# Two early tiles leave the six rotating PSUM banks, and the opening order is written anew

## The chip, the cores and the metric

The kernel runs on one core of one Trainium2 chip. The metric is the device time of one execution in microseconds (us), the median of three runs. A profile is one more execution, taken by the hardware profiler; its span runs from the first to the last instruction. The engines: TensorE (PE for matmuls, PEld for the weight loads that go beside them), VectorE (DVE), ScalarE (ACT), GpSimd (POOL), and SyncE (SP), which here only issues DMAs.

## The reference

A gated recurrence over 768 positions, for 4 batches and 8 heads, feeds a two-layer feed-forward network of 3072 tokens:

```
# recurrence, in chunks of 32: L[i,j] = exp(cum_i - cum_j) for i >= j, else 0
y_intra = (C @ B.T * L) @ x
y_inter = (C @ state) * exp(cum)
state   = exp(sum(log a)) * state + (B * exp(cum_last - cum)).T @ x
# network, d_model 256, d_ff 2048, on the recurrence's output
h   = y @ w_in
out = softplus(h) @ w_out
```

## The kernel before

**Tiling.** The positions are cut into 6 units u of 128, for all batches. A unit becomes 512 tokens of the network. The network's hidden side is cut into 16 slices k of 128. For each of the 96 pairs (j, k) there is a *first* (F: six matmuls of 512 columns, `w_in` times x, into a PSUM tile `hp`), then ACT's Softplus into `e`, its high part `gh` (ACT) and the rest `gl` (DVE), and a *second* (Z: two times three matmuls into the accumulators `acc0`, `acc1`). All network products are split into high and low float32r parts, three matmuls for each product.

**The recurrence of a unit.** Each unit has two halves p. The words of one half: D (four decay masks `rm`, written by POOL from factors `fc`), S (scores, PE, four PSUM tiles `sp`), M (four products of `sp` and `rm`, DVE), I (within, PE, into `yp`). Then B, U, T, N carry the state, C and R read it, G multiplies `yp` by growths `gg` (DVE), Xh and Xl split the result into `xh` (ACT) and `xl` (DVE), which the firsts read. H1 and H0 are halves of unit 0's first two F, that need only half of its tokens.

**Weights.** A word w*n* loads 512 KB of raw weights (SP); six words W*n* turn them into high and low parts, with four steps on ACT (`w`, two of `signs`, `wih` or `woh`) and two on DVE (`w`, `wil` or `wol`). Four buffers `wraw` hold the raw weights, so that a later load waits until ACT has read an earlier one.

**Order.** Nearly everything up to the 32nd F and the 28th Z is a list of words, `ORDER` (line 61), replayed with every instruction kept in its engine's order; later units are placed by `FILLS`. Each engine works through its own queue in order and waits on semaphores.

**PSUM.** There are eight banks. Six belong to the pool `ps` (line 129) and rotate under one tag: `zeros`, `fp`, `total`, `log_sums`, `sp`, `hp` and others take the next free one. Two belong to `pa` (line 130): the accumulators `acc0` and `acc1`, which unit 0's `yp` and two of the growths' tiles borrow through `early_bank` (line 213) before the first Z.

**The opening.** `la`, `lb`, `kb` load logs and constants; `loga` takes logarithms; `ft0` multiplies them by summing matrices (`fp0` and `total0`, lines 321 to 339) and exponentiates into `fc` and `ft`; `warm` (line 298) issues matmuls of zeros into `zeros`; `gc` and `gq` make unit 0's growths on chip (`log_sums`, `by_head_row`, `gp`); `gd` and `gg1` take the other units' growths through DRAM; `us` and `ux` load the rows and tokens of unit 0, `un` those of a later one.

Of the kernel before, what the change touches and what calls it, by code (L numbers as in the profile page):

```python
# [10 lines left out]
F32 = mybir.dt.float32  # L11
# [10 lines left out]
P = 128  # L22
# [36 lines left out]


ORDER = """
la loga lb logr warm6 loga ft0 logr ft0 ft0 warm1 ft0 ft0 ft0 kb growth logb gb D0.0.0 growth gc us0.0 w0 S0.0 D0.0.1
gc warm1 M0.0.0 W0 ux0.0 D0.0.2 M0.0.2 gq M0.0.1 D0.0.3 us0.1 M0.0.3 fr0 W0 gq B0.0 W0 logb ux0.1 D0.1.0 warm1 gq
growth gq fr0 W0 W0 I0.0 S0.1 ft1 w2 B0.1 D0.1.3 G0.0 gq fr0 M0.1.0 Xh0.0 D1.0.2 D0.1.1 M0.1.3 ft1 D0.1.2 M0.1.1
M0.1.2 D1.0.3 ft1 fr1 fr1 un1.0 U0 W2 W0 w4 Xl0.0 fr0 I0.1 w1 ft1 G0.1 W2 W2 D1.1.0 fr1 W2 N0 S1.0 W4 fr1 Xh0.1 W4 H1
D1.0.1 Xl0.1 H0 M1.0.1 D1.1.3 W2 W2 M1.0.2 W4 F0.1 W4 tl F0.0 W1 W4 gd P0.0 F0.2 un1.1 D1.0.0 P0.2 M1.0.0 w6 W1 T1
F0.3 P0.1 M1.0.3 w3 D1.1.2 S1.1 W1 B1.0 P0.0 B1.1 P0.1 W4 M1.1.0 W1 W1 un2.0 F0.5 W3 P0.2 D1.1.1 P0.0 W1 F0.4 P0.5 W3
M1.1.1 P0.1 Z0.0 gg1 M1.1.2 W6 Z0.1 M1.1.3 W6 W3 W6 P0.4 C1 P0.5 P0.2 P0.4 W3 U1 P0.3 W3 w7 I1.0 W6 N1 w5 I1.1 W3 R1
W6 G1.0 w12 Xh1.0 W6 G1.1 W7 P0.3 P0.3 S2.0 Z0.2 F0.7 w9 W5 W7 W7 D2.0.0 M2.0.0 Xh1.1 un3.0 w8 F0.6 W5 P0.4 Xl1.0
Xl1.1 W5 Z0.3 D2.0.3 P0.6 M2.0.3 W5 W5 B2.0 D2.0.1 W5 F1.4 P0.6 F1.0 Z0.4 P0.7 M2.0.1 un2.1 F1.7 F1.1 F1.3 P0.7 W7 W8  # L70
P0.5 W7 P1.0 W7 W12 Z0.5 B2.1 F1.2 w10 W8 P0.6 W8 W12 W12 P1.0 P1.1 P0.7 Z0.6 Z0.7 P1.4 W12 W12 P1.4 P1.1 P1.0 F1.5
K0.1 P1.1 P1.2 K0.0 W12 W8 D2.0.2 P1.2 W8 W8 P1.4 Z1.0 F1.6 P1.5 Z1.1 W10 W10 W9 W10 P1.2 P1.6 W10 F0.9 W10 P1.5 w14
P1.7 W10 P1.5 P1.3 Z1.2 P1.3 P1.3 W9 D2.1.2 P1.7 W9 P1.7 W9 W9 W9 P0.9 T2 F0.10 C2 F0.13 P0.13 W14 Z1.3 P0.13 Z1.4 w11
W11 W11 P1.6 P1.6 W11 W11 F0.12 D2.1.0 w15 F0.11 W14 W14 w13 F0.8 Z1.5 W14 W11 P0.13 W11 W14 P0.12 P0.9 W14 F1.8 P0.10
P0.9 W13 P0.8 Z1.6 F1.12 F0.14 P0.10 P0.10 P0.14 W13 W15 Z1.7 F0.15 P0.8 P0.8 F1.13 K1.1 K1.0 W13 W15 W13 W15 M2.0.2
W15 P0.11 W15 Z0.8 Z0.9 gg2 W13 P0.11 Z0.10 P0.14 P0.14 W15 P0.15 F1.9 F1.10 P0.11 P0.12 P1.9 W13 P0.12 Z0.11 Z0.12
P0.15 P1.9 D3.0.0 P1.10 P1.9 Z0.13 P0.15 P1.8 P1.8 Z0.14 Z0.15 P1.10 E0 D2.1.1 F1.14 D2.1.3 F1.11 D3.0.2 P1.8 P1.12
P1.14 Z1.8 P1.14 S2.1 P1.10 M2.1.3 M2.1.1 M2.1.0 Z1.9 M2.1.2 P1.12 U2 P1.11 P1.11 P1.14 N2 P1.12 P1.13 I2.0 I2.1 P1.11
S3.0 M3.0.0 R2 G2.1 D3.0.1 Z1.10 G2.0 M3.0.1 P1.13 M3.0.2 Xh2.1 F1.15 P1.13 un3.1 Xl2.1 D3.0.3 Z1.11 Xh2.0 P1.15 P1.15
Xl2.0 M3.0.3 gg3 P1.15  # L80
"""
HALF = NFT // 2
AHEAD = 32
# [37 lines left out]
def recurrence_then_ffn(ctx: ExitStack, tc: tile.TileContext, un, alr, w_in, w_out, const, outT):  # L121
# [7 lines left out]
    ps = ctx.enter_context(tc.tile_pool(name="ps", bufs=6, space=PSUM))  # L129
# [30 lines left out]
    kb = cp.tile([P, C_END], F32, name="kb")  # L160
# [8 lines left out]
    gd = dr.tile([NH, NU * RT], F32, name="gd")  # L169
# [43 lines left out]
    def early_bank(e, name):  # L213
        return pa.tile([P, 512], F32, tag=f"acc{e}", name=name)
# [81 lines left out]
    zeros = []  # L296

    def warm(n):
        if not zeros:
            zeros.append(ps.tile([P, 512], F32, tag="ps", name="zeros"))  # L300
        for _ in range(n):
            PE.matmul(
                zeros[0][:32].rearrange("p (a b) -> p a b", b=32),
                some,
                some.unsqueeze(1).broadcast_to([P, 16, 32]),
                start=True,
                stop=True,
            )
# [12 lines left out]
    def factors_by_token(g):  # L321
        logs = first_logs[:, : NS * NR] if g == 0 else lo
        n = logs.shape[1]
        fp = ps.tile([P, 512], F32, tag="ps", name=f"fp{g}")
        for i in range(NC):
            PE.matmul(fp[:, i * n : (i + 1) * n], kc[:, i * P : (i + 1) * P], logs, start=True, stop=True)
        yield
        by_chunk = fp[:, : NC * n].rearrange("p (c k) -> p c k", c=NC)
        total = None
        for a, b in ((0, NR), (NR, n)) if g == 0 else ((0, n),):  # L330
            cols = slice(g * NS * NR + a, g * NS * NR + b)
            A.activation(fc[:, cols].rearrange("p k c -> p c k"), by_chunk[:, :, a:b], AF.Exp)
            yield
            if total is None:
                total = ps.tile([P, 512], F32, tag="ps", name=f"total{g}")[:, :n]
                PE.matmul(total, kc[:, NC * P : K_END], logs, start=True, stop=True)
                yield
            A.activation(ft[:, cols], total[:, a:b], AF.Exp)
            yield
# [408 lines left out]
    def constants_on_chip():  # L748
# [3 lines left out]
    acts = {  # L752
        "init": constants_on_chip,
        "warm": warm,
        "la": lambda: load(first_logs, alr[:, : (NS + 1) * NR]),
        "lb": lambda: load(other_logs, alr[:, (NS + 1) * NR :]),
# [12 lines left out]
        "logr": staged(lambda: log_clipped(lr)),  # L769
        "growth": staged(growth),  # L770
        "ft": staged(factors_by_token),
        "fr": staged(factors_by_row),
        "W": staged(split_stages),
# [112 lines left out]
```

## Time and profile before

| | us |
|---|---|
| runs, median of 3 (lowest to highest) | 313.52 (313.27 to 314.02) |
| profiled execution | 313.66 |
| its span, first to last instruction | 312.0 |
| PE busy (98% of the span) | 307.1 |
| ACT busy (54%) | 169.0 |
| DVE busy (50%) | 154.7 |
| POOL busy (13%) | 41.5 |

The engines other than PE do most of their work in the first third: the tenths of ACT's busy time are 9 in slices 4 to 6 of 40 and fall to 3 and 4 after slice 18. A matmul's end is modelled, so the time between the starts of neighbouring matmuls tells more than a busy share of 9 or 10 tenths.

### The profile page before, as it was taken

How to read it: one execution, taken by the hardware profiler on the slowest of the kernel's cores; microseconds unless marked ns; L12 is line 12 of the kernel's file. 1: busy time of each engine (PE TensorE's matmuls, PEld its weight loads, DVE VectorE, ACT ScalarE, POOL GpSimd, SP SyncE). 2: the span in 40 equal slices, each digit the busy share in tenths (PEclk: the TensorE clock that was granted, in tenths of full speed). 3: DMA queues.
4: the chain of work that ended last, by engine and by line, in shares of the span. 5: the costliest groups of instructions: out<-in, count | busy, mean ns of one | idle time of the engine just before them, and what ended most of it. 6: DMA issues, size and time to landing. Idle time of an engine off the chain costs nothing.

```text
span 312.0 us, 5683 instructions
## 1 busy us (share of the span) xinstructions
PE 307.1 (98%) x2325; PEld 251.9 (81%) x2325; DVE 154.7 (50%) x264; ACT 169.0 (54%) x292; POOL 41.5 (13%) x55
## 2 busy tenths in 40 slices
PE   8999999999999999999999999999999999999995
PEld 5787888888788888888888888888888888888884
DVE  5999793647444973553922252642352332322222
ACT  4899897988855254244344534344534344534450
POOL 2780600004410531000300000300000000000000
PEclk9999999999999999999999999999999999999999
DMA  7997664240004550000610100000100000100001
GB/s 214 406 373 178 237 235 137 63 137 2 2 0 152 165 193 35 35 1 2 237 35 0 69 0 0 4 0 0 67 4 0 2 0 2 67 0 0 2 0 67
DMA packets 10442, 24.37 MB, mean 78 GB/s; under 512 B 1072, under 2 KB 1840, under 8 KB 10416
## 3 DMA queue, kind: packets, MB, share of 16 engines
q1 hardware_dynamic: 10416, 24.01, 22.9%
q8 instruction: 18, 0.29, 0.4%
q14 instruction: 8, 0.07, 0.1%
HBM read 20.76 MB, written 3.24 MB: 77 GB/s over the span
## 4 chain that ended last, share of the span: by engine, by line
PE 91%; ACT 3%; DVE 3%; issue 1%; POOL 1%; POOLq 0%; DVEq 0%; ACTq 0%
PE acc L141 40%; PE hp L141 39%; PE yp L141 5%; PE sp L141 4%; ACT signs L141 1%; PE zp L141 1%; PE end L141 1%; DVE rm L141 1%; PE zeros L141 1%; DVE gl L141 1%; ACT gh L141 1%; PE fp L141 1%; ACT e L141 1%; POOL rm L141 1%; DVE wil L141 0%
## 5 line engine op out<-in xcount | busy, mean ns | idle before, releaser
L655 DVE TENSOR_TENSOR gl<-e,gh 128x512 fp32r<-128x512 f32 x54 | 37.3, 692 | 92.0 <-ACT gh L652 92.0
L141 PE MATMUL hp<-xh,wih 128*128 128x512 f32 (+1 forms) x196 | 75.7, 386 | 0.0
L141 PE MATMUL hp<-xl,wih 128*128 128x512 f32 (+1 forms) x196 | 75.4, 385 | 0.0
L141 PE MATMUL hp<-xh,wil 128*128 128x512 f32 (+1 forms) x196 | 75.4, 385 | 0.0
L141 PE MATMUL acc<-gh,woh 128*128 128x512 f32 x188 | 74.3, 395 | 0.1
L649 ACT ACTIVATE e<-hp 128x512 f32<-128x512 f32 x54 | 32.3, 599 | 77.6 <-PE hp L141 77.3
L141 PE MATMUL acc<-gl,woh 128*128 128x512 f32 x188 | 73.3, 390 | 0.0
L141 PE MATMUL acc<-gh,wol 128*128 128x512 f32 x188 | 73.2, 389 | 0.0
L141 DVE TENSOR_TENSOR gl<-e,gh 128x512 fp32r<-128x512 f32 x42 | 30.3, 731 | 32.8 <-ACT gh L141 32.8
L141 PEld LDWEIGHTS hp<-xh,wih 128*128 128x128 f32 x196 | 36.8, 188 | 7.5
L141 PEld LDWEIGHTS hp<-xh,wil 128*128 128x128 f32 x196 | 36.8, 188 | 7.4
L141 PEld LDWEIGHTS hp<-xl,wih 128*128 128x128 f32 x196 | 36.8, 188 | 7.3
L141 POOL TENSOR_SCALAR_AFFINE_SELECT rm<-fc 128x512 f32<-128x512 f32 x36 | 32.2, 929 | 77.0 <-ACT signs L141 41.9
L141 PEld LDWEIGHTS acc<-gh,woh 128*128 128x128 f32 x188 | 35.3, 188 | 8.7 <-ACT signs L141 0.5
L141 PEld LDWEIGHTS acc<-gh,wol 128*128 128x128 f32 x188 | 35.3, 188 | 7.4
L141 PEld LDWEIGHTS acc<-gl,woh 128*128 128x128 f32 x188 | 35.3, 188 | 7.2 <-DVE gl L655 0.2
L141 ACT ACTIVATE e<-hp 128x512 f32<-128x512 f32 x42 | 24.6, 592 | 22.0 <-PE hp L141 17.3
L652 ACT CAST gh<-e 128x512 fp32r<-128x512 f32 x54 | 33.5, 621 | 4.1 <-PE acc L141 2.4
L141 ACT CAST gh<-e 128x512 fp32r<-128x512 f32 x42 | 25.6, 616 | 12.9 <-PE acc L141 12.4
L141 DVE TENSOR_TENSOR rm<-sp,rm 128x512 f32<-128x512 f32 x32 | 20.7, 683 | 5.3 <-PE sp L141 5.2
L141 ACT ACTIVATE signs<-wraw 128x512 f16<-128x512 f32 (+1 forms) x32 | 23.3, 781 | 0.0
L405 POOL TENSOR_SCALAR_AFFINE_SELECT rm<-fc 128x512 f32<-128x512 f32 x12 | 8.7, 754 | 81.4 <-PE yp L141 69.4
(105 smaller groups left out, 209.5 us busy)
## 6 DMA issues: line engine op xcount, KB each, us to landing
un<-in_un SPq DMA_DIRECT2D x10, 768.0 KB, 6.0
wraw<-in_w_in SPq DMA_DIRECT2D x8, 512.0 KB, 5.2
wraw<-in_w_out SPq DMA_DIRECT2D x8, 512.0 KB, 5.3
gg<-gd SPq DMA_DIRECT2D x20, 128.0 KB, 3.8
out_t<-o SPq DMA_DIRECT2D x9, 256.0 KB, 2.1
head_in_h<-in_un SPq DMA_DIRECT2D x2, 384.0 KB, 4.9
head_in_l<-in_un SPq DMA_DIRECT2D x2, 384.0 KB, 6.3
out_t<-half SPq DMA_DIRECT2D x2, 256.0 KB, 2.2
```

The costliest lines, as they stand in the source:

```text
L141: return lambda *a, **k: tc.keep_in_program_order(f(*a, **k))
L405: Pl.affine_select(out=weights_of(u, p, ks.start, ks.stop).rearrange("p h (c i) -> p (h c) i", i=SUB), in_=fs.rearrange("p h c -> p (h c)" ...
L649: A.activation(e, h, AF.Softplus)
L652: A.copy(gh, e)
L655: V.tensor_tensor(gl, e, gh.bitcast(F32), op=ALU.subtract)
```

## The change

`zeros` and `total0` are taken from the two accumulator banks instead of the six rotating ones, and the word list is another one. The nine matmuls of zeros all stand ahead of `gq`, since `gp0` takes the bank of `zeros`. Line 335 (the second factors' `total1`) stays in the rotating pool.

```diff
 ORDER = """
-la loga lb logr warm6 loga ft0 logr ft0 ft0 warm1 ft0 ft0 ft0 kb growth logb gb D0.0.0 growth gc us0.0 w0 S0.0 D0.0.1
...
+warm6 la loga lb loga logr logb ft0 logr us0.0 growth growth kb gb ft0 ft0 ft0 ft0 S0.0 ft0 D0.0.0 w0 M0.0.0 gc gc
...
     def warm(n):
         if not zeros:
-            zeros.append(ps.tile([P, 512], F32, tag="ps", name="zeros"))
+            zeros.append(early_bank(0, "zeros"))
...
             if total is None:
-                total = ps.tile([P, 512], F32, tag="ps", name=f"total{g}")[:, :n]
+                total = (ps.tile([P, 512], F32, tag="ps", name="total1") if g else early_bank(1, "total0"))[:, :n]
                 PE.matmul(total, kc[:, NC * P : K_END], logs, start=True, stop=True)
```

From unit 3 on (`FILLS`), and in the last 798 rows of PE's queue, both programs have the same order. Three places of the new order matter below.

The first is the opening on PE and DVE. Before, on PE, from the first factors' `total` to the first scores (`sp` of unit 0, first half, four tiles):

```order
L141 MATMUL total_124<-first_logs,kc 128x128
L141 LDWEIGHTS some
L141 MATMUL zeros<-some 32x512
L141 MATMUL log_sums<-kc,first_logs 32x128 x4
L141 MATMUL sp_00_148<-head_in_h 128x128
L141 MATMUL sp_01_149<-head_in_h 128x128
L141 MATMUL sp_02_150<-head_in_h 128x128
L141 MATMUL sp_03_151<-head_in_h 128x128
```

Now, on PE, the end of those scores and what follows them:

```order
L141 MATMUL sp_00_137<-head_in_h 128x128
L141 MATMUL sp_01_138<-head_in_h 128x128
L141 MATMUL sp_02_139<-head_in_h 128x128
L141 MATMUL sp_03_140<-head_in_h 128x128
L141 MATMUL log_sums<-kc,first_logs 32x128 x4
L141 LDWEIGHTS some
L141 MATMUL zeros<-some 32x512
```

The scores now come straight behind `total`; `log_sums` and three matmuls of zeros (of which the first stands here) moved behind them. On DVE, before, around the same scores (`by_head_row` reads `log_sums`; the four rows of `rm` are the words M0.0):

```order
L141 SCALAR_TENSOR_TENSOR other_logs<-cum 128x192
L141 COPY by_head_row<-log_sums 128x128
L141 TENSOR_TENSOR rm_0_137<-sp_00_148,rm_0_137 128x512
L141 TENSOR_TENSOR rm_0_137<-sp_02_150,rm_0_137 128x512
L141 TENSOR_TENSOR rm_0_137<-sp_01_149,rm_0_137 128x512
L141 TENSOR_TENSOR rm_0_137<-sp_03_151,rm_0_137 128x512
```

And now:

```order
L141 COPY own<-kb 128x256
L141 TENSOR_TENSOR rm_0_158<-sp_00_137,rm_0_158 128x512
L141 COPY by_head_row<-log_sums 128x128
L141 TENSOR_TENSOR rm_0_158<-sp_01_138,rm_0_158 128x512
L141 TENSOR_TENSOR rm_0_158<-sp_02_139,rm_0_158 128x512
L141 TENSOR_TENSOR rm_0_158<-sp_03_140,rm_0_158 128x512
```

`by_head_row` moved from ahead of the four products to behind the first of them.

The second place is POOL, from unit 1's first mask on (`rm0_1` is unit 0's second half, `rm1_0` and `rm1_1` are the halves of unit 1). Before:

```order
L141 AFFINE_SELECT rm1_0_270<-fc_90 128x512
L141 AFFINE_SELECT rm0_1_204<-fc_90 128x512 x2
L141 AFFINE_SELECT rm1_0_270<-fc_90 128x512
L141 AFFINE_SELECT rm1_1_333<-fc_90 128x512
L141 AFFINE_SELECT rm1_0_270<-fc_90 128x512
L141 AFFINE_SELECT rm1_1_333<-fc_90 128x512
L141 AFFINE_SELECT rm1_0_270<-fc_90 128x512
L141 AFFINE_SELECT rm1_1_333<-fc_90 128x512 x2
```

And now:

```order
L141 AFFINE_SELECT rm1_0_233<-fc_90 128x512
L141 AFFINE_SELECT rm0_1_195<-fc_90 128x512 x2
L141 AFFINE_SELECT rm1_0_233<-fc_90 128x512
L141 AFFINE_SELECT rm1_1_363<-fc_90 128x512 x2
L141 AFFINE_SELECT rm1_0_233<-fc_90 128x512 x2
L141 AFFINE_SELECT rm1_1_363<-fc_90 128x512 x2
```

The last two masks of `rm1_0` are now third and fourth of the six that wait for unit 0's second `yp`; before they were second and fourth. The fourth is D1.0.3, which M1.0.3 reads.

The third place is SP's loads, after unit 1's second half (`un`, the 768 KB of a half unit; `wraw` from `in_w_out`, an odd w). Before:

```order
L150 DMA un_285<-in_un 128x1536
L150 DMA wraw_419<-in_w_in 128x2x512
L150 DMA wraw_434<-in_w_out 128x2x512
L150 DMA un_470<-in_un 128x1536
L150 DMA gg_508<-gd 32x2x512 x4
```

And now:

```order
L150 DMA un_265<-in_un 128x1536
L150 DMA gd<-other_logs 128x192
L150 DMA un_428<-in_un 128x1536
L150 DMA wraw_459<-in_w_out 128x2x512
L150 DMA gg_503<-gd 32x2x512 x4
```

The load of w3 (`in_w_out`) moved behind unit 2's half, and w6 (`in_w_in`) stands earlier, ahead of w1. At the very start, the rows `us0.0` are now the third load and the constants `kb` the fourth; before it was the other way round.

## Rows read from the trace of the kernel before

**Rows 1.** Busy time by stretch: window, PE, PEld, DVE, ACT, POOL, clock, DMA share, GB/s.
```profile
25.00:30.00 5.00, 5.00 (x23) 4.12 (x23) 4.91 (x9) 4.99 (x10) 0.00 (x0) 1.00 0.77 209
50.00:60.00 10.00, 10.00 (x46) 8.29 (x45) 5.04 (x9) 7.69 (x14) 0.00 (x0) 1.00 0.22 74
80.00:90.00 10.00, 9.86 (x44) 7.87 (x43) 6.29 (x10) 8.18 (x15) 4.54 (x5) 1.00 0.01 2
```

**Rows 2.** Chain that ended last, first 18 us and a later piece: start, us, what.
```profile
6.41 0.76 ACT fc L141
7.17 0.04 issue
7.21 1.17 PE sp L141 x21
...
9.57 1.29 DVE rm L141 x2
10.86 0.04 issue
10.90 0.87 PE yp L141 x20
...
11.89 1.62 POOL rm L141 x2
...
13.55 1.29 DVE rm L141 x2
14.84 0.04 issue
14.88 0.65 PE zp L141 x32
15.54 0.87 PE yp L141 x32
16.41 0.34 PE rp L141 x2
16.75 1.11 PE sp L141 x32
...
50.12 1.36 PE hp L141 x6
```

**Rows 3.** Timeline of the opening: start, us, engine, line, operation, count, idle before.
```profile
5.54 0.64 PE L141 MATMUL total<-first_logs,kc 128*128 128x128 f32 x2
...
6.25 4.12 POOL L141 TENSOR_SCALAR_AFFINE_SELECT rm<-fc 128x512 f32<-128x512 f32 x6 [4.94 <-ACT fc L141]
...
6.64 0.30 PEld L141 LDWEIGHTS sp<-head_in_h 32*128 32x128 f32 x4 [0.20 <-DMA head_in_h<-in_un]
...
6.80 0.29 DVE L141 COPY by_head_row<-log_sums 128x128 f32<-128x128 f32 x1 [1.44 <-PE log_sums L141]
...
8.36 2.48 DVE L141 TENSOR_TENSOR rm<-sp,rm 128x512 f32<-128x512 f32 x4 [1.27 <-PE sp L141]
...
8.69 1.12 PE L141 MATMUL gp<-by_head_row,own 32*128 32x128 f32 x16
...
11.89 2.97 POOL L141 TENSOR_SCALAR_AFFINE_SELECT rm<-fc 128x512 f32<-128x512 f32 x4 [1.51 <-PE yp L141]
...
12.94 2.48 DVE L141 TENSOR_TENSOR rm<-sp,rm 128x512 f32<-128x512 f32 x4
```

**Rows 4.** Timeline, POOL's masks after unit 0's second `yp`, and a later wait.
```profile
16.51 2.00 POOL L141 TENSOR_SCALAR_AFFINE_SELECT rm<-fc 128x512 f32<-128x512 f32 x2 [1.65 <-PE yp L141]
...
17.27 5.69 POOL L141 TENSOR_SCALAR_AFFINE_SELECT rm<-fc 128x512 f32<-128x512 f32 x5
...
33.95 0.86 DVE L141 TENSOR_TENSOR wol<-w,woh 128x512 fp32r<-128x512 f32 x1 [1.08 <-ACT woh L141]
```

**Rows 5.** Timeline where the accumulators change hands.
```profile
82.07 0.68 DVE L141 COPY half<-acc 128x512 f32<-128x512 f32 x1
...
82.37 0.39 PE L141 MATMUL hp<-xh,wil 128*128 128x512 f32 x1
...
82.87 0.19 PEld L141 LDWEIGHTS acc<-gh,woh 128*128 128x128 f32 x1 [0.53 <-ACT signs L141]
82.90 0.47 PE L141 MATMUL acc<-gh,woh 128*128 128x512 f32 x1
```

**Rows 6.** Timeline around the load of w3: its issue, the use, zp of unit 1.
```profile
16.57 0.38 SPq L150 DMA_DIRECT2D wraw<-in_w_out  x1
...
26.65 0.67 ACT L141 ACTIVATE w<-wraw 128x512 f32<-128x512 f32 x1
...
30.38 0.65 PE L141 MATMUL zp<-un,bp 128*32 128x64 f32 x32
```

**Rows 7.** Transfers of raw weights, shortest, median and longest (view by tile).
```profile
DMA to landing us min/median/max: 3.5/5.3/10.9
```

More of the change, by code (lines that the diff above doesn't have):

```diff
@@ L61 @@
 ORDER = """
-la loga lb logr warm6 loga ft0 logr ft0 ft0 warm1 ft0 ft0 ft0 kb growth logb gb D0.0.0 growth gc us0.0 w0 S0.0 D0.0.1
[L63 to L80, printed above, removed]
+warm6 la loga lb loga logr logb ft0 logr us0.0 growth growth kb gb ft0 ft0 ft0 ft0 S0.0 ft0 D0.0.0 w0 M0.0.0 gc gc
+D0.0.1 M0.0.1 D0.0.2 M0.0.2 warm1 warm1 W0 warm1 W0 D0.0.3 gq gq D0.1.0 ux0.0 gq fr0 M0.0.3 W0 us0.1 fr0 B0.0 ux0.1 gq
@@ new lines @@
+W0 I0.0 G0.0 D0.1.2 B0.1 D1.0.0 logb W0 Xh0.0 S0.1 M0.1.0 w2 gq growth un1.0 ft1 ft1 fr0 fr0 D0.1.1 ft1 M0.1.2 W2 fr1
+M0.1.1 D0.1.3 M0.1.3 U0 fr1 Xl0.0 W0 I0.1 fr1 W2 ft1 D1.0.2 w4 S1.0 W2 fr1 H1 G0.1 W4 D1.1.1 Xh0.1 D1.1.3 W2 w6 W4 w1
+N0 Xl0.1 M1.0.0 W2 H0 F0.0 W4 W2 D1.0.1 D1.0.3 tl F0.1 un1.1 M1.0.3 M1.0.2 W4 gd W1 P0.1 F0.2 P0.2 M1.0.1 F0.3 un2.0
+S1.1 B1.0 P0.0 W4 W4 W1 W1 M1.1.1 w3 F0.4 P0.0 W1 W1 P0.0 W1 W6 B1.1 P0.1 P0.2 W3 F0.5 P0.5 W6 P0.1 C1 D1.1.2 D1.1.0
+W3 gg1 Z0.0 M1.1.0 M1.1.3 W3 P0.2 W6 w5 Z0.1 M1.1.2 P0.4 P0.3 W3 W6 T1 U1 I1.0 D2.0.1 W3 w10 N1 D2.0.0 I1.1 R1 W3 G1.0
@@ new lines @@
+W6 S2.0 G1.1 Z0.2 D2.0.2 Xh1.0 P0.5 W6 W5 W5 M2.0.1 F0.6 P0.3 w7 W7 W5 M2.0.0 M2.0.2 P0.3 T2 W7 F0.7 Z0.3 Xl1.0 D2.1.2
+w12 P0.5 Xh1.1 Xl1.1 W5 W7 F1.0 P0.6 W5 W5 P1.0 F1.1 W7 P0.4 F1.6 P0.4 Z0.4 W10 F1.2 W10 W10 P1.1 W10 P0.6 Z0.5 P1.0
+P0.6 P0.7 W7 W7 F1.3 Z0.6 w11 w14 P0.7 P1.1 W10 P1.1 W12 W12 P1.0 W12 w8 P0.7 W10 W12 Z0.7 B2.0 P1.3 W14 W14 K0.1
+D2.0.3 W14 W12 M2.0.3 F1.4 W12 W8 F1.10 un2.1 P1.2 P1.6 F0.11 W14 K0.0 C2 F1.5 F0.10 w13 Z1.0 Z1.1 w9 P1.2 P1.3 P1.2
+W8 W8 W14 W14 F1.7 un3.0 P1.4 Z1.2 P1.6 W8 W8 W11 P1.6 W8 P1.4 F0.8 W9 W9 P1.5 un3.1 P1.3 W9 Z1.3 W11 P1.7 P1.7 P1.4
@@ new lines @@
+Z1.4 W9 W11 P0.11 W11 W9 P1.5 F1.9 P1.5 F0.9 P0.11 Z1.5 P1.7 w15 W9 P0.8 P0.9 W15 W11 W15 Z1.6 W15 gg2 W15 W11 Z1.7
+K1.0 P0.9 P0.9 F0.15 P0.8 W13 F1.12 K1.1 W13 W13 W15 P0.8 W13 Z0.8 B2.1 P0.15 W13 P0.11 P0.10 F0.12 W13 P0.10 F1.8
+F0.14 Z0.9 gg3 P0.14 P0.10 P0.12 P0.12 Z0.10 W15 P0.12 Z0.11 F0.13 F1.15 P0.15 P0.13 D3.0.2 D2.1.3 P0.14 P0.13 P0.14
+Z0.12 P0.13 P0.15 P1.9 Z0.13 P1.15 P1.8 P1.8 P1.8 D2.1.1 F1.11 P1.15 P1.15 Z0.14 Z0.15 D2.1.0 E0 P1.9 P1.9 P1.12 P1.10
+S2.1 M2.1.1 F1.14 P1.14 M2.1.0 M2.1.3 M2.1.2 Z1.8 P1.10 P1.10 P1.11 P1.11 D3.0.1 U2 N2 I2.0 I2.1 S3.0 M3.0.1 M3.0.2
@@ L81 @@
+P1.11 R2 G2.1 D3.0.3 G2.0 M3.0.3 Xh2.0 F1.13 Xh2.1 Xl2.1 Z1.9 Z1.10 D3.0.0 M3.0.0 P1.14 Xl2.0 Z1.11 P1.12 P1.14 P1.12
+P1.13 P1.13 P1.13
 """
```

## The prediction

> **What bounds the kernel now.** I read the busy time by stretch first. The reader is to see that PE is full in every stretch from 25 us on, 46 matmuls in the ten microseconds from 50 on, and that only the stretch from 80 on has fewer, 44, and a busy time below 10.00 [rows 1]. DVE and ACT lie well below PE there, but not in 25 to 30 us, where DVE has 4.91 and ACT 4.99 of 5.00 [rows 1]. Next comes the chain of waits. Up to 17.86 us (16.75 + 1.11, where the first *firsts* begin) it goes back and forth: PE's scores, DVE's products with the masks, PE's `yp`, POOL's next masks, DVE again, then PE alone. Behind that it is almost all PE, six matmuls of 512 columns in 1.36 us, 0.227 from start to start [rows 2]. The timeline of the opening gives each of these steps its wait [rows 3], and a timeline at 82 us shows the one later gap: a matmul starts at 82.37, the next at 82.90, where 82.60 was due, since its weights wait for the banks whose halves DVE and ACT copy out [rows 5]. That is 0.30 us.
>
> So the profiled execution, 313.66 us, is 17.86 us of opening, PE's fixed work, and 0.30 us of stall in the middle. The change adds no matmul and removes none: PE's sum stays, and the last 798 rows of its queue are the same. It can win or lose only where PE waits. The profiled execution lies 0.14 us above the median of the runs, 313.52, so I take the sum off the median as well.
>
> **The change part by part.** *Scores of unit 0's first half.* The chain shows ACT's exponential `fc` from 6.41 to 7.17 and then the last 21 score matmuls from 7.21 [rows 2]. The scores themselves had begun at 6.64, when their rows landed [rows 3], so 11 of 32 ran and the third tile waited. Six rotating banks held zeros, `fp0`, `total0`, `log_sums` and two score tiles; the third tile needed the bank that `fc` was reading. With zeros and `total0` in the accumulators' banks, and `log_sums` behind the scores, four score tiles have a bank at once. What is late next: `total` ends at 6.18 (5.54 + 0.64), and the rows, whose load is now ahead of `kb` (issue some 0.47 us earlier, a slot of SP's queue), should land at 6.2 to 6.4 instead of 6.6 [rows 3]. I take 6.3. 32 scores take 1.11 to 1.17 us [rows 2], so they end at 7.45, where before it was 8.38: 0.9 us earlier. The first mask is there by then: POOL makes six in 4.12 us from 6.25, 0.69 each, the first at 6.94 [rows 3].
>
> *DVE's products.* `by_head_row`, 0.29 us, lay in DVE's idle time (1.27 us before the first product) and cost nothing [rows 3]. Now it stands between the first product and the second, on the path. A product takes 0.62 us (2.48 for four): 7.45 to 8.05, the copy to 8.34, three more to 10.20. Before, they ended at 10.84, so 0.64 of the 0.9 is left. The three matmuls of zeros behind `log_sums` end by about 8.4, at 0.23 each, beside DVE's products; if that cover is gone, they cost at most 0.7.
>
> *From there to the first firsts.* `yp` ends 0.87 us later [rows 2] plus its start, at about 11.1; POOL's next masks start at 11.2 instead of 11.89. DVE does the same 2.10 us of other work between its groups (10.84 to 12.94) and starts the next products at 12.3 [rows 3]. ACT now makes two growths ahead of a step of W0 that DVE waits for; I price that at 0 to 0.15 and take 0. The products end at 14.78. Before, `zp` waited for DVE until 14.88 [rows 3], with 1.87 us of PE's own rows behind it (0.65 + 0.87 + 0.34 with joints) up to the scores at 16.75 [rows 2]. In the new order `zp` stands ahead of that wait and needs only ACT's factors, which by my walk are there near 14.0. So `yp` follows the last product directly, at 14.8 at the earliest, or PE's own rows at 14.7: `yp` to 15.6, `rp` 0.34, scores 1.11, and the first firsts at 17.05 to 17.15. That is 0.75 us earlier than 17.86. PE's later waits keep their slack if DVE and ACT come 0.7 us earlier too, which they do in this walk.
>
> *The gap at 82 us.* In the new order the copies of the halves come right behind the last *second* of token tile 1, and the work that stood in front of them on ACT and DVE is done some 1.5 to 2 us before PE needs the banks. The 0.30 us go [rows 5].
>
> *The rest of the new order* (weights' steps, the loads, unit 1's masks) moves words among each other. Where PE's next word needs them, my walk by the rows' durations finds every one in time, but three with under 0.5 us to spare: unit 1's scores of its second half (0.2), unit 2's scores (0.15), and the first *seconds*, which wait for `wol` (0.45). An example of what such a wait looks like stands at 33.95, where DVE stood 1.08 us for ACT's `woh` [rows 4]. I count them at 0, and bound them by 0 below (PE is full, so nothing can be won) and some 0.9 us above, the delay of one mask, below.
>
> The sum: −0.75 − 0.30 = −1.05, from 313.52 to 312.5.
>
> **The rivals.** *B: DVE stands for a mask and the gain of the opening is partly given back.* Unit 1's fourth product M1.0.3 now waits for D1.0.3, the fourth of POOL's masks behind unit 0's second `yp`, where M1.0.1 waited for an earlier one. Masks cost 0.69 each at 6.25 us, 0.74 at 11.89, but 1.00 and 1.14 in the two groups at 16.51 and 17.27 [rows 3, 4]. From 15.8 on, four at 0.76 to 1.24 are done at 20.1, while DVE would be free at 19.3: 0.85 us of idle time in a queue that is nearly full in 25 to 30 us [rows 1]. Behind it are M1.0.1, which frees the bank of unit 1's next scores, and the steps of W1. Slacks of 0.15 to 0.45 then go under by 0.4 to 0.7: 312.9 to 313.4, mid 313.1. Against it: W and P words can be late without PE noticing at most places. The Trainium skill, "SBUF — State Buffer", section "SBUF: two separate sides", says that VectorE and GpSimd share a pair of ports as an exclusive lock, and that a VectorE operation with two SBUF inputs blocks a GpSimd operation that reads SBUF. The rows bear it out in kind: 0.69 us beside products that read PSUM, 1.14 us beside steps that read SBUF alone [rows 3, 4]. By that rule a DVE that stands still for the mask lets POOL run at 0.69, and the mask would be there at about 19.6, so B's wait would be 0.35 us and its end 312.7; no run here shows it yet.
>
> *C: the opening's gain doesn't reach PE.* The scores come earlier, but DVE or ACT, which have W0, growths and factors of their own in the same stretch, hold the second products where they were; only the 0.30 us are won: 313.2. For it: ACT's and DVE's queues at 25 to 30 us [rows 1]. Against it: all of the chain's steps to 17.86 hang on the score's start [rows 2].
>
> *D: slower, by the load of w3.* It was issued at 16.57, ahead of unit 2's 768 KB, and ACT read it at 26.65 [rows 6]. Now it stands behind those 768 KB, and ACT reads it first at about 26 to 28. The longest of these transfers took 10.9 us from issue to landing, the median 5.3 [rows 7]. Issued at 15.9, it lands at 21.2 by the median and at 26.8 by the longest, in time. If it took a third longer than the longest shown, some 14.6 us, and landed at 30.5, ACT stands with `e` of later firsts behind it, `zp` of unit 1 waits for the bank that such an `e` reads, and starts at 31.6 where 30.38 is shown [rows 6]: +1.2 on the old clock of the opening, −0.30 at 82 us, 314.4. The point from which it decides is a landing behind 28.1.
>
> *E: more.* DVE takes the 0.7 us and PE finds the scores at 6.2, no growth delays W0, and the tight places stay clear: 1.3 to 1.6 us off, 312.0.
>
> **How the numbers follow.** Forecast A, 312.5 (its own range 312.2 to 312.85): 0.44. B, 313.1: 0.24. C, 313.2: 0.11. D, 314.4 (314.0 to 314.8): 0.12. E, 312.0: 0.09. A change under 0.2%, 0.63 us, can't be told from none here; so faster is below 312.9 and slower above 314.15. Faster holds A, E and a quarter of B (312.7 to 312.9): 0.59. Slower is most of D: 0.10. The rest, C, most of B and D's edge, is the same: 0.31. For 8 in 10 the range reaches from E's better half, 311.8, to D's lower edge, 314.1; it leaves out most of D and a little of E. It holds cases of one sign for the most part.
>
> **What the profile of the changed kernel would show.** Right: the scores of unit 0 without a wait for `fc` between them; the first product at about 7.45; the copy `by_head_row` behind it; the first `hp` at about 17.1; no weight load that waits for the accumulators near 78 us. B: DVE idle before a product, ended by POOL, at 19 to 20 us, and PE idle before scores at 23 or 33 us. C: the first `hp` at 17.7 or later although the scores were early. D: ACT idle before `w`, ended by a DMA, at 27 to 30 us, and `zp` of unit 1 behind 31. The prediction is wrong in its first term if the scores wait on, for rows that land at 6.6 or for a bank; and in the second if a gap appears at another change of the accumulators.

## The result: slower by 2.6 us

The changed kernel takes 316.14 us, median of 6 runs (315.75 to 316.46), against 313.50 for the kernel before in the same comparison (313.22 to 314.02). The ratio is 1.0081, interval 1.0070 to 1.0093. The forecast was 312.5, the range 311.8 to 314.1. The profiled execution took 316.08 us with a span of 314.4, so 2.4 us more in the profile.

The busy time by stretch of the changed kernel comes first (window, PE, PEld, DVE, ACT, POOL, clock, DMA share, GB/s):

```profile
25.00:30.00 5.00, 5.00 (x34) 3.90 (x36) 4.86 (x10) 4.58 (x9) 0.00 (x0) 1.00 0.68 218
30.00:40.00 10.00, 9.16 (x179) 7.77 (x172) 9.88 (x17) 7.38 (x14) 4.52 (x5) 1.00 0.32 107
70.00:80.00 10.00, 9.78 (x44) 7.76 (x42) 6.97 (x8) 7.47 (x14) 6.75 (x7) 1.00 0.00 0
80.00:90.00 10.00, 9.55 (x42) 7.92 (x43) 5.55 (x8) 5.43 (x10) 2.09 (x2) 1.00 0.01 2
110.00:120.00 10.00, 9.29 (x41) 7.35 (x40) 5.32 (x9) 4.62 (x8) 1.08 (x2) 1.00 0.34 115
```

PE is still full from 25 to 30 us, as in [rows 1]. Three stretches have holes: 30 to 40, 78 to 82, and 110 to 120 us. In the kernel before the first and the last of them were full, and near 82 us there was only the gap of [rows 5]:

```profile
30.00:40.00 10.00, 10.00 (x185) 8.25 (x185) 8.34 (x16) 8.99 (x17) 5.22 (x6) 1.00 0.55 186
110.00:120.00 10.00, 10.00 (x46) 8.28 (x45) 5.59 (x9) 4.95 (x9) 1.88 (x3) 1.00 0.31 118
```

The starts of PE's words in the two timelines give the ledger; a word's time "to the next word" runs from its first matmul to the first matmul of the word behind it. The first `hp` starts 1.05 us earlier (16.74 against 17.79). F0.2, the first whole first behind the split ones, starts only 0.54 earlier (20.23 against 20.77), and so do unit 2's scores (33.20 against 33.74). Those scores then take 2.39 us to the next word instead of 1.10, which loses 1.29. A *second* that waits for nothing takes 1.36; Z0.8 takes 2.33 (0.97 lost), and Z1.12 takes 2.37 (1.01 lost). The gap at 82 us [rows 5] is gone: from Z1.7 to Z0.8 it is 4.08 instead of 4.38 (0.30 won). The sum is −0.54 + 1.29 + 0.97 + 1.01 − 0.30 = 2.43; the last 798 rows of PE's queue, behind all of these, start 2.42 later. (Two terms of 0.10 cancel: Z0.8 took 1.46 before, and F1.0 takes 1.47 now.)

The opening in the timeline of the changed kernel (start, us, engine, line, operation, count, idle before):

```profile
5.79 1.17 PE L141 MATMUL sp<-head_in_h 32*128 32x128 f32 x32
...
9.39 0.85 PE L141 MATMUL yp<-rm,head_in_h 128*32 128x128 f32 x20 [0.31 <-DMA head_in_h<-in_un]
...
16.29 0.70 ACT L141 ACTIVATE w<-wraw 128x512 f32<-128x512 f32 x1 [0.34 <-DMA wraw<-in_w_in]
16.74 0.39 PE L141 MATMUL hp<-xh,wih 128*128 128x256 f32 x1
16.88 0.63 ACT L141 CAST xh<-gg 128x512 fp32r<-128x512 f32 x1
17.51 0.72 POOL L141 TENSOR_SCALAR_AFFINE_SELECT rm<-fc 128x512 f32<-128x512 f32 x1
17.54 1.23 DVE L141 TENSOR_TENSOR xl<-gg,xh 128x512 fp32r<-128x512 f32 x1 [0.24 <-ACT xh L141]
18.82 0.39 PE L141 MATMUL hp<-xl,wih 128*128 128x256 f32 x1 [0.26 <-DVE xl L141]
```

The scores run without a break: 32 in 1.17 us, where before they took from 6.64 to 8.38 with a wait for `fc` [rows 2, 3]. The `yp` behind them now waits for its tokens. The new wait is at 18.82, in F0.0, the word behind H1 and H0: it is the first that needs the other half of the tokens, and so their `xl`. (The expectations below call it H0's wait.) `xl` comes late for two reasons. It stands behind ACT's `xh`, which stands behind ACT's first step of w4, which waited for the load. And it takes 1.23 us, 0.54 more than such a step takes elsewhere, since a mask of POOL had started 0.03 us ahead of it. Without that 0.54 it would have been there at about 18.25, an estimate from these rows, ahead of 18.40, when PE wanted it. The run with `td` alone shows this (e11, below).

Unit 2's scores, on three engines:

```profile
31.01 1.80 DVE L141 SCALAR_TENSOR_TENSOR w<-w,signs 128x512 int32<-128x512 int32 x2
31.52 4.52 POOL L141 TENSOR_SCALAR_AFFINE_SELECT rm<-fc 128x512 f32<-128x512 f32 x5 [10.28 <-PE yp L141]
32.73 0.93 DVE L141 TENSOR_TENSOR td<-tb,fr 128x256 f32<-128x256 f32 x1
33.20 0.50 PE L141 MATMUL sp<-un 32*128 32x128 f32 x6
33.77 0.61 DVE L141 SCALAR_TENSOR_TENSOR tb<-zp,kb,td 128x128 f32<-128x128 f32 x2
34.53 1.12 PE L141 MATMUL sp<-un 32*128 32x128 f32 x26 [0.83 <-DVE tb L141]
```

The fourth score tile needs the bank that `tb` reads (`zp` of unit 1). In front of `tb` stand two `w`, of which the second takes 1.2 us, and `td`, 0.93 us, both while POOL makes masks. In the kernel before, `td` had been made ten microseconds earlier, both `w` were over in 1.29 us, and `tb` stood right behind them, 1.47 us ahead of the scores at 33.74:

```profile
21.97 0.41 DVE L141 TENSOR_TENSOR td<-tb,fr 128x256 f32<-128x256 f32 x1
...
31.06 1.29 DVE L141 SCALAR_TENSOR_TENSOR w<-w,signs 128x512 int32<-128x512 int32 x2
32.27 0.60 DVE L141 SCALAR_TENSOR_TENSOR tb<-zp,kb,td 128x128 f32<-128x128 f32 x2
```

Z0.8, on three engines:

```profile
76.32 3.56 POOL L141 TENSOR_SCALAR_AFFINE_SELECT rm<-fc 128x512 f32<-128x512 f32 x3 [3.12 <-ACT signs L141]
76.89 1.20 DVE L141 TENSOR_TENSOR wol<-w,woh 128x512 fp32r<-128x512 f32 x1
78.01 0.68 DVE L141 COPY half<-acc 128x512 f32<-128x512 f32 x1
78.61 1.79 DVE L141 TENSOR_TENSOR gl<-e,gh 128x512 fp32r<-128x512 f32 x2
79.39 0.39 PE L141 MATMUL acc<-gh,woh 128*128 128x512 f32 x1
80.45 0.50 PE L141 MATMUL acc<-gl,woh 128*128 128x512 f32 x1 [0.67 <-DVE gl L141]
```

PE's second matmul of Z0.8, due at 79.62, waits for the second of the two `gl` at 78.61. That is `gl` of (0,8), put behind `gl` of (0,9), which PE needs only at 85.8. Again `wol` and one `gl` take 1.2 us beside masks.

Z1.12:

```profile
107.13 1.29 DVE L141 TENSOR_TENSOR rm<-sp,rm 128x512 f32<-128x512 f32 x2 [2.26 <-POOL rm L141]
108.34 0.80 DVE L141 TENSOR_TENSOR gl<-e,gh 128x512 fp32r<-128x512 f32 x1
109.06 1.28 DVE L141 TENSOR_TENSOR gg<-yp,gg 128x512 f32<-128x512 f32 x2
110.36 1.14 ACT L141 CAST xh<-gg 128x512 fp32r<-128x512 f32 x2 [4.97 <-DMA un<-in_un]
...
113.35 1.89 DVE L141 TENSOR_TENSOR gl<-e,gh 128x512 fp32r<-128x512 f32 x3
...
114.69 0.50 PE L141 MATMUL acc<-gl,woh 128*128 128x512 f32 x1 [0.70 <-DVE gl L141]
```

Here no step takes 1.2 us; the slowest `gl` takes 0.80. Two products of unit 3 (M3.0.1, M3.0.2) stand in front of a `gl` and of unit 2's `gg`, and hold DVE for 2.26 us. The releaser named, POOL, is not the one: their masks were made at 69 to 80 us, and what ends last before 107.13 is unit 3's scores on PE. The same holds for ACT's `xh`: it starts as the second `gg` ends. Of the three `gl` at 113.35, the second, that of (1,12), is the one that PE waits for; the first is that of (1,14), which PE needs later, so the order has here the fault that it has at Z0.8. Turned round, some 0.6 of this wait would go, an estimate from the length of a `gl`; no run does this alone.

### The profile page after: what moved, and what is told of

It is laid out like the page before. It is cut to its first block, busy times and chain, and to the rows that moved or that the text cites. A ratio compares the mean times of both kernels' runs of the same rounds, so it can differ in the third digit from the quotient of the medians.

```text
span 314.4 us, 5688 instructions
## 1 busy us (share of the span) xinstructions
PE 307.2 (98%) x2325; PEld 251.3 (80%) x2325; DVE 157.6 (50%) x264; ACT 168.5 (54%) x292; POOL 41.3 (13%) x55
## 4 chain that ended last, share of the span: by engine, by line
PE 81%; DVE 6%; DMA 5%; ACT 4%; issue 2%; SPq 0%; POOL 0%; DVEq 0%; ACTq 0%; POOLq 0%
PE acc L141 36%; PE hp L141 36%; PE yp L141 3%; PE sp L141 3%; DMA gd<-other_logs 3%; DVE gl L141 2%; DVE rm L141 1%; DMA un<-in_un 1%; DMA gg<-gd 1%; ACT signs L141 1%; ACT gh L141 1%; PE end L141 1%; PE zeros L141 1%; DVE w L141 1%; DVE wol L141 1%
```

## The experiments

All times are compared with the kernel before on the same chip (313.67 to 313.72). In the edits a line is a piece of the word list.

**The banks alone** (e1).

```
 (with the diff of the two banks)
-M0.0.2 gq M0.0.1 ... D0.1.0 warm1 gq
+M0.0.2 warm1 gq M0.0.1 ... D0.1.0 gq
```

> The bank change alone, with the old word list (only the last matmul of zeros is moved ahead of the first growths, as the banks need it). My theory (Q: the opening's gain is real, and it was lost to waits that the new word list makes later): the third score tile no longer waits for fc, but rows us0.0 still land behind kb, so scores run from 6.64 without a break; the first hp at 17.3 to 17.6, the 0.30 us gap at 82 us stays, 312.9 to 313.3. Rival (S: what comes earlier at the start runs into engines and loads that are full and gains nothing): 313.5 within 0.2, the first hp early but the time given back by 36 us.

Measured 313.41 us, ratio 0.9996 (0.9986 to 1.0007). The time is S's and not Q's, but the profile shows nothing that was given back: the first `hp` was at 17.13, Z0.0 at 26.89, and no new wait behind it. The bank change costs nothing; what it gives is not clear of zero.

**The new opening, the old remainder** (e2).

```
 (changed kernel's words up to H1)
-G0.1 W4 D1.1.1 Xh0.1 D1.1.3 W2 w6 W4 w1 ...
+D1.0.3 w1 G0.1 D1.1.0 W2 N0 W4 Xh0.1 W4 D1.0.1 ...   (the old list's order to the end)
```

> The changed kernel's opening (bank change, and its words up to H1), then the remaining words in the order of the kernel before. Q: the first hp at 16.7 to 16.9 as in the changed kernel, no wait at unit 2's scores, at Z0.8 or at Z1.12, the gap of 0.30 at 82 us stays: 312.4 to 312.9. S: some of the 1.05 us comes back as waits between 17 and 36 us on DVE, ACT or a load: 313.2 or more.

Measured 313.03 us, ratio 0.9983 (0.9973 to 0.9994). The first `hp` was at 16.44, but PE stood 0.46 us for `xl` at 18.56 (1.13 us long, again beside a mask), and Z0.0 started at 26.77, hardly before the banks alone. Unit 2's scores, Z0.8 and Z1.12 had no wait of their own; the gap of 0.30 in front of Z0.8 stays. So the loss sits in the words behind H1, and in this profile part of the opening's gain goes at that `xl` even with the old remainder. The time lies between Q's and S's.

**Four moves in the changed kernel** (e3).

```
-G0.1 W4 D1.1.1 Xh0.1
+G0.1 Xh0.1 W4 D1.1.1
-P0.2 M1.0.1 F0.3 ... T1 U1
+P0.2 M1.0.1 T1 F0.3 ... U1
-K1.0 P0.9 P0.9 F0.15 P0.8 W13 F1.12 K1.1 W13 W13 W15 P0.8
+K1.0 P0.8 P0.8 F0.15 P0.9 W13 F1.12 K1.1 W13 W13 W15 P0.9
-S3.0 M3.0.1 M3.0.2 P1.11 R2 G2.1 D3.0.3 G2.0 M3.0.3
+S3.0 P1.11 R2 G2.1 D3.0.3 G2.0 M3.0.1 M3.0.2 M3.0.3
```

> The changed kernel with four moves in its word list and nothing else: Xh0.1 ahead of the first step of W4; T1 (td) from behind unit 1's zp work to behind M1.0.1; the gh and gl of (0,8) ahead of those of (0,9) behind K1.0; M3.0.1 and M3.0.2 behind G2.0. Q: the waits of 0.5 us at H0, 1.3 at unit 2's scores, 0.9 at Z0.8 and 1.0 at Z1.12 shrink to 0.1, 0.3, 0 and 0, so 312.2 to 313.2, faster than both. Rival L (the chain of waits names the loads of gd, gg1 and of w3, which now come later): the loads stand as in the changed kernel, so the wait at unit 2's scores stays at 0.8 or more and the time is 313.6 to 314.5. If the waits merely move on to the next place, 314.5 to 316.

Measured 313.92 us, ratio 1.0011 (1.0001 to 1.0020): 2.2 us less than the changed kernel, but not the 312.2 to 313.2 that Q expected. The timeline of PE:

```profile
33.27 1.40 PE L141 MATMUL sp<-un 32*128 32x128 f32 x32
...
106.80 0.50 PE L141 MATMUL hp<-xh,wih 128*128 128x512 f32 x1 [0.81 <-DVE gg L141]
```

The scores run in 1.40 us, the waits at Z0.8 and Z1.12 are gone, and so is F0.0's. In their place F1.13 waits 0.81 for the bank of `yp`, which `gg` now frees last. L's time fits, but its mark, a wait of 0.8 or more at unit 2's scores, is not there: the loads' order did not make that wait.

**Masks that read nothing** (e4).

```
+        if u == 2 or (u, p) == (3, 0):
+            Pl.memset(weights_of(u, p, ks.start, ks.stop), 1.0)
+            return
         Pl.affine_select(
```

> The changed kernel, but POOL's twelve masks of unit 2 and of unit 3's first half are memsets of the same tiles (POOL writes them and reads nothing; the masks' values are left out of the computation). Theory M (a POOL mask that reads SBUF holds up DVE operations with two SBUF inputs; those are the 1.2 us steps beside the masks where 0.69 is usual): DVE's w at 31.6 takes 0.6 and td 0.35, wol and gl at 77 to 80 take 0.6; the wait at unit 2's scores falls from 1.2 to at most 0.3 and the one at Z0.8 from 0.9 to 0, that at Z1.12 stays: 314.0 to 314.6. Rival (queue order alone makes these waits, the slow steps are not due to the masks): 316.1 within 0.3.

Measured 313.84 us, ratio 1.0010 (1.0000 to 1.0019): 2.3 us less than the changed kernel, with its word list untouched, and a little below M's 314.0 to 314.6. The timeline of DVE and POOL:

```profile
30.86 1.28 DVE L141 SCALAR_TENSOR_TENSOR w<-w,signs 128x512 int32<-128x512 int32 x2
31.36 2.39 POOL L141 MEMSET rm<- 128x512 f32 x5 [9.96 <-PE yp L141]
32.06 0.42 DVE L141 TENSOR_TENSOR td<-tb,fr 128x256 f32<-128x256 f32 x1
...
74.51 1.46 POOL L141 MEMSET rm<- 128x512 f32 x3 [4.84 <-ACT signs L141]
75.09 0.69 DVE L141 TENSOR_TENSOR wol<-w,woh 128x512 fp32r<-128x512 f32 x1
...
76.30 1.28 DVE L141 TENSOR_TENSOR gl<-e,gh 128x512 fp32r<-128x512 f32 x2
```

Beside POOL's memsets the DVE steps take their usual time: `wol` 0.69 instead of 1.20 us, `td` 0.42 instead of 0.93. Unit 2's scores take 1.36 us to the next word, Z0.8 its natural 1.36, and Z1.12 keeps its wait (2.36), as M said. The Trainium skill, "SBUF — State Buffer", section "SBUF: two separate sides", says that of a VectorE operation with two SBUF inputs and a GpSimd operation that reads SBUF, whichever starts first locks the other out until it is done. The trace agrees, 1.20 against 0.69 us, in the direction that the prediction left out: here it is DVE that waits. At Z0.8, too, either cure is enough: e3 moved the `gl` and left the masks, this run left the `gl` and took the masks away, and both have 1.36.

**The same memsets in the kernel before** (e7), the same edit.

> The kernel before, with the same twelve masks as memsets that read nothing (their values left out). Theory M (masks cost the changed kernel 2.2 us because its order puts DVE steps that PE waits for beside them, and the old order has slack there): steps beside the masks take 0.69 instead of 1.2 here too, but PE gains at most the 0.3 at 82 us: 313.2 to 313.8. Rival (memsets help any order, for less work on POOL and DVE): 311.5 to 312.5.

Measured 313.24 us, ratio 0.9983 (0.9975 to 0.9992). First two DVE steps of the kernel before, beside masks, then the same two here:

```profile
73.17 1.20 DVE L141 TENSOR_TENSOR gl<-e,gh 128x512 fp32r<-128x512 f32 x1
74.29 1.19 DVE L141 TENSOR_TENSOR wol<-w,woh 128x512 fp32r<-128x512 f32 x1
```

```profile
72.39 0.68 DVE L141 TENSOR_TENSOR gl<-e,gh 128x512 fp32r<-128x512 f32 x1
72.99 0.68 DVE L141 TENSOR_TENSOR wol<-w,woh 128x512 fp32r<-128x512 f32 x1
```

These are M's numbers. The lock is as long in the old order, but PE waits for none of these steps; only the gap at 82 us goes. The masks' price is a matter of what stands beside them.

**td alone** (e11).

```
-P0.2 M1.0.1 F0.3 ... T1 U1
+P0.2 M1.0.1 T1 F0.3 ... U1
```

> The changed kernel with T1 (td) alone moved, from behind unit 1's zp work to behind M1.0.1; the masks run as they did. If td's place in the queue is enough: the wait at unit 2's scores falls from 1.2 to 0.3 or 0.4, the waits at Z0.8 and Z1.12 stay at 0.9 each: 315.0 to 315.4. If only the masks beside w and tb count: the wait stays at 0.8 or more, 315.7 to 316.2.

Measured 314.69 us, ratio 1.0034 (1.0022 to 1.0046). Its timeline at unit 2's scores:

```profile
30.89 1.79 DVE L141 SCALAR_TENSOR_TENSOR w<-w,signs 128x512 int32<-128x512 int32 x2
32.60 0.60 DVE L141 SCALAR_TENSOR_TENSOR tb<-zp,kb,td 128x128 f32<-128x128 f32 x2
32.87 1.60 PE L141 MATMUL sp<-un 32*128 32x128 f32 x32
```

The scores take 1.53 us to the next word instead of 2.39, so `td` at that place was worth 0.86 of the 1.29; the slow `w` in front of `tb` is still there. Either cure, `td` elsewhere or masks that don't read, takes most of this wait: the wait needs both causes.

The time is 0.3 below the range. In its profile one more wait was gone, that of F0.0, though no word near it had moved:

```profile
17.63 0.69 DVE L141 TENSOR_TENSOR xl<-gg,xh 128x512 fp32r<-128x512 f32 x1 [0.16 <-ACT xh L141]
17.68 1.23 POOL L141 TENSOR_SCALAR_AFFINE_SELECT rm<-fc 128x512 f32<-128x512 f32 x1
```

ACT's `xh` started at 16.98, even later than in the changed kernel (16.88). But here `xl` started 0.05 us ahead of the mask, took 0.69 us, and PE did not wait; it was the mask that took 1.23.

**The second wait of e3** (e6).

```
-M3.0.3 Xh2.0 F1.13 Xh2.1 Xl2.1 Z1.9 Z1.10
+M3.0.3 Xh2.0 Xh2.1 Xl2.1 Z1.9 F1.13 Z1.10
```

> The kernel of the run with four moves (313.92 us), with F1.13 moved behind Z1.9, so that it needs its bank (read by G2's products) 1.4 us later. Theory Q (the wait of 0.88 at F1.13 is the one that took the place of Z1.12's): it goes, nothing new comes, 312.9 to 313.3. Rival (it moves on again): 313.6 to 314.2, with a wait of 0.5 or more between 107 and 116 us.

Measured 313.17 us, ratio 0.9992 (0.9979 to 1.0005). F1.13's wait is gone. Of Z1.12's, 0.58 us came back (1.94 to the next word), so it moved on in part. The opening came through whole here: the first `hp` at 16.54, F0.2 at 19.50, Z0.0 at 26.31, 9.77 us behind the first `hp` as in the kernel before (9.78).

**Xh0.1 first, and the copies earlier** (e5), on top of e2.

```
-W4 Xh0.1 W4
+Xh0.1 W4 W4
-W15 Z1.7 F0.15 P0.8 P0.8 F1.13 K1.1 K1.0 W13 W15
+Z1.7 F0.15 P0.8 K1.1 K1.0 P0.8 F1.13 W15 W13 W15
```

> The kernel of the run with the changed opening and the old remainder (313.03 us), with two moves: Xh0.1 ahead of the first step of W4 on ACT, and at 80 us gh of (0,8), then the two copies of the halves (K1), ahead of gl and of w15's first step. Theory W (the opening's gain is capped because ACT's first step of W4 waits for w4 to land near 16.1, with Xh0.1 queued behind it, and H0 waits for the xl that follows): H0's wait of 0.46 shrinks to 0.1, Z0.0 starts at 26.3 to 26.5 where five kernels so far had 26.8 to 27.1, the gap of 0.30 at 82 us goes: 312.1 to 312.6. Rival (DVE's slow xl beside POOL's mask, 1.13 to 1.23 us instead of 0.68, sets H0 alone, or unit 1's scores take over the wait): Z0.0 stays at 26.7 or later, only the gap goes, 312.7 to 312.9.

Measured 312.90 us, ratio 0.9977 (0.9962 to 0.9993), the rival's numbers. The wait for `xl` is gone, but unit 1's scores take it over:

```profile
22.71 1.61 PE L141 MATMUL sp<-un 32*128 32x128 f32 x32
```

and

```profile
21.53 0.60 ACT L141 CAST wih<-w 128x512 fp32r<-128x512 f32 x1
22.04 1.07 ACT L141 ACTIVATE e<-hp 128x512 f32<-128x512 f32 x2
```

The last score tiles need the banks that ACT's `e` read, at 22.04 and 22.52, and ACT has worked without a break since 16.60. Z0.0 started at 27.12. That is a matter of the old remainder, which puts `wih` ahead of these `e`: in e6, with Xh0.1 moved in the changed kernel's own list, ACT makes the `e` first, at 21.03, and unit 1's scores have no wait.

**The new words with the old banks** (e8): e2's word list, without the diff of the banks.

> The kernel with the changed opening and the old remainder (313.03 us), but zeros and total0 in the rotating banks as before: the new word order without the bank change. Theory W (the opening is capped at H0 by w4's load and xl, so most of what the scores win is lost there): the scores of unit 0 wait for fc again, the first hp comes at 17.2 to 17.8, but Z0.0 at 26.9 to 27.4 and 313.1 to 313.5. Rival (the scores' wait carries through to the end): 313.8 to 314.1.

Measured 313.39 us, ratio 0.9994 (0.9983 to 1.0005): theory W's numbers. The scores wait 0.6 for `fc` again and the first `hp` comes at 17.29, 0.85 later than in e2, but Z0.0 only 0.30 later, at 27.07, since nothing waits between the two (9.78 us against e2's 10.33). Against e2 the intervals overlap, so what the banks give to the new opening isn't clear of the noise either.

**The copies alone** (e10), on the kernel before, the second edit of e5.

> The kernel before with one move: gh of (0,8), then the copies of the halves (K1), ahead of gl and of w15's first step, at 80 us. If the term of 0.30 us is right: no gap between the firsts and Z0.8, 313.2 to 313.5, ratio 0.9985 to 0.9995. If another wait (gl of (0,8), or w15 later on) takes its place: ratio 1.000 or more, with an idle PE near 82 us or behind 90 us.

Measured 313.23 us, ratio 0.9984 (0.9974 to 0.9993). The place that answers to [rows 5]:

```profile
82.22 0.39 PE L141 MATMUL hp<-xh,wil 128*128 128x512 f32 x1
82.44 0.39 PE L141 MATMUL acc<-gh,woh 128*128 128x512 f32 x1
```

0.22 from start to start instead of 0.53: the term of 0.30 was right, within the interval of 0.2 to 0.8 us that the runs leave.

**Joined** (e9): the changed kernel's words with Xh0.1 and T1 moved as in e3, up to Z0.1, then the old list, with e10's move.

> The changed kernel's words with Xh0.1 and T1 moved, up to Z0.1 at about 28 us, then the remaining words of the kernel before, with the copies of the halves (K1) moved up at 80 us. Theory Q (early part of the one and later part of the other, neither with a wait behind 17 us): Z0.0 at 26.3 to 26.7, unit 2's scores without a wait, no gap at 82 us, 312.2 to 312.7, ratio 0.996 to 0.998. Rival (ACT or the masks make a new wait at the joint, 28 to 40 us): 313.0 to 314.0.

Measured 312.85 us, ratio 0.9974 (0.9963 to 0.9984), faster than both kernels, with Q's ratio and a time 0.15 above Q's range. Z0.0 was at 26.91, with no wait since the first `hp` at 17.14, and unit 2's scores took 1.57 us to the next word: 0.47 are lost at the joint, beside the masks, as the rival had it in kind.

## Why the prediction was wrong

**The opening, −0.75.** Right in mechanism, and near in size at the first `hp`: 16.44 to 17.33, mean 16.89, in the eight profiles with the new words up to H1 and the new banks (the changed kernel, e2 to e6, e9, e11), against 17.79, 17.64 and 17.03 with the old ones (before, e10, e7), mean 17.49, so −0.60; the two sets overlap. (One reading was wrong without harm to the sum: not 11 of the 32 scores but four had started before 7.21, as the x4 in [rows 3] says.) The sentence that failed is that PE's later waits keep their slack if DVE and ACT come 0.7 earlier too. From the first `hp` to Z0.0 PE needs 9.77 us when nothing waits. It took 10.28 in the changed kernel and 10.33 in e2: some 0.5 us were lost at one `xl`, which is late behind ACT's `xh` and beside a mask. With `xh` ahead of w4's step (e3, e6, e9) it is 9.77, and so it is where the mask started behind `xl` (e11). Of C, which had the gain stop at DVE or ACT, the mark was not seen: the first `hp` was at 16.74 and not at 17.7.

**The gap at 82 us, −0.30.** Right, and e10 shows it alone. But that the work in front of the copies "is done some 1.5 to 2 us before PE needs the banks" was followed for the banks only: Z0.8 also reads `gl` of (0,8), which the new list put behind that of (0,9). That cost 0.97, three times what the place was to give.

**The walk that "finds every one in time, but three", bounded by 0.9 us.** This is the step that made the sign wrong. Unit 2's scores were one of the three, with 0.15 to spare, but the price was 1.29, and Z0.8 and Z1.12 were not among them. The walk itself is not on record; the prediction's rows show steps of DVE with 0.62 to 0.86 us and none with 1.2, though the trace of the kernel before has them (73.17, shown under e7). Beside POOL's masks a step with two inputs from SBUF takes 1.2, and the masks start when their buffers come free, so which steps they hit depends on the list. Twelve masks made into memsets take 2.3 us off the changed kernel and 0.4 off the kernel before: the same lock, with and without a PE that waits. Z1.12's 1.01 is not of this kind: e4 leaves it as it was, and no step there takes 1.2; it is the order of DVE's queue.

**The lock in the prediction.** The lock was named, but only as something that makes masks late (rival B); its other side, DVE's own steps made late, stood in no term of the sum.

**The rivals.** B: DVE did not stand for D1.0.3, and unit 1's scores did not wait. PE did stand at the scores at 33 us, as B's marks had it, but for `tb` behind slow steps of DVE and not for a product that waits for its mask. D: `zp` of unit 1 started at 29.84, earlier than in [rows 6], and ACT did not wait for w3. So the slower case was foreseen with the wrong mechanism. Not settled is how much of Z1.12's wait would go with a list that moves nothing else: e3 and e6 each moved a part of it on, and none puts `gl` of (1,12) ahead of that of (1,14).

## What to carry to other kernels

When an order is changed, walk the engine that PE waits for with the durations that its steps have beside their new neighbours: here a VectorE step with two inputs from SBUF, 0.69 us by itself, took 1.2 when a GpSimd mask had started ahead of it. Follow every operand of the word that is to start earlier, not only the one whose wait is removed. An opening that ends earlier is worth what the steps behind it let through: in the changed kernel 1.05 us at the first `hp` became 0.54 at the first whole *first*, for one `xl`, and with one cast of ACT moved forward nothing was lost on that way (e6).

## What the runs showed of the hardware

The same opening code put the first `hp` at 17.03, 17.64 and 17.79 us in three profiled executions (e7, e10, before), as its scores began at 6.09, 6.60 and 6.65 with the landing of their rows. The kernel before ran from 312.82 to 314.30 us in 35 runs beside the first four experiments. A gain of a few tenths in the opening is less than what one execution's loads can shift.

Which of two steps pays for the lock goes by which starts first, and hundredths of a microsecond decide it: a mask that started 0.03 us ahead of `xl` took 0.72 and `xl` 1.23 (the changed kernel), and an `xl` that started 0.05 us ahead of the mask took 0.69 and the mask 1.23 (e11). A step of DVE that reads PSUM, the copy `half` at 78.01, kept its 0.68 us beside a mask.
